# Raw words of w_out and of the last network loaded from POOL's queue, with earlier scalings and reads of h

## The chip, the cores and the metric

The kernel runs on one core of a Trainium2 chip. The metric is device time in microseconds. The core's engines each work through their own list of instructions in order: PE multiplies, DVE, ACT and POOL work element by element, SP does nothing but issue DMAs here. In the profile "SPq" is SP's queue and PEld the loading of weights into PE.

## What is computed

The reference, cut to what matters:

```python
# q, k, v: (4, 8, 576, 64), f: (4, 8, 576); all matrices of weights are float64
cum = cumsum(log(clip(f, 1e-4, 1)))
s = q @ k.T / 8 + cum[i] - cum[j]            # causal, -1e9 above the diagonal
p = exp(s - max(s)); p = p / (sum(p) + 1e-9)
x = (p @ v)                                  # as 2304 tokens x 512
h = x @ w_in                                 # 512 -> 2048
z = mish(h) @ w_out                          # 2048 -> 512
out = max(z @ w1, z @ w2, z @ w3) @ w_out2   # 512 -> 768 -> 512
```

## The kernel before

**Arithmetic.** Matmuls run in a reduced format, so each operand is split into a high and a low part and mm3 makes three products of them (lines 177 to 179: L177 is high by high, and so on for all matmuls of the networks). The weights lie in DRAM as float64. load_f32 brings their raw words (tile wr, or wr1 for the last network) by SP's queue (L150), and five DVE steps (L155 to L166) make float32 of them (tile wt; for w_in ACT does the first step). Then a split writes high and low part: for w_in on ACT and POOL, for all others on POOL alone (L138 the high, L142 the low). This whole is called a conversion below: 16 for w_in, 16 for w_out, 24 for w1 to w3, 6 for the last w_out. For w_in and w_out the raw words have two buffers, for the last network one.

**Attention.** Sixteen pairs of heads are worked through, each in three parts that overlap with the neighbours'. load() reads k, q, v and the decay rows (tile cb) and lets POOL mask cb (L285, L293). prep() splits and transposes q and k (tr). scores() multiplies them (sc), finds the row minima on DVE (mn), takes the exponential on ACT (L398), adds up and inverts the row sums on DVE (rr, L402, L403), and scales P on POOL (L405). av() transposes P (pp, L424), splits it (TA, TB) and multiplies by v (av); the result xt goes to DRAM (x_d, L462). A pair is done in two halves, g = 0 and g = 1.

**First network.** x_d is read in nine blocks of 256 tokens, split on POOL (xh, xl), and multiplied by w_in in 72 "h steps" of 24 matmuls; as many of them as are ready run between the parts of attention. ACT or DVE copies the result out of PSUM (he, L527 or L525), SP stores it (h_d, L529). In the "y phase" load_g reads h back (g, L610), applies Mish on ACT (L611) and splits it (gh on ACT, gl on DVE); 80 "y steps" of 12 matmuls by w_out add up y, which is copied to ze and stored as z_d. Two reads of h are asked for ahead of the step that uses them.

**Last network.** z_d is read (yr), split (yh, yl), and multiplied by w1, w2, w3 (tile wm; product g); the maximum goes to mx, is split (hh, hl) and multiplied by wo2 into o, copied to oe and stored.

**Order.** The order of the code is only a start: a scheduler that simulates the program arranges each engine's list. Work in a high_priority block is taken earlier, by the block's number; AHEAD is 3000. w_in is converted by a generator that the loop over attention calls (two conversions for each of the calls 7 to 14), those of w_out by the loop of the remaining h steps, and those of the last network by every second y step.

Of the kernel before, what the change touches and what calls it, by code (L numbers as in the profile page):

```python
# [32 lines left out]
BLK = 256  # L33
# [34 lines left out]
def tile_decay_attention__mish_ff__max3_ff(  # L68
# [38 lines left out]
    make_identity(nc, ident)  # L107
    identr = const.tile([128, 128], F32R, name="identr")
    nc.vector.tensor_copy(identr, ident)
# [33 lines left out]

    def load_f32(pool, srcs, bufs=None, abs_eng="dve", raw="wr"):

        m, n = len(srcs), srcs[0].shape[1]
        t = pool.tile([128, m, n], F32, name="wt", tag="wt", bufs=bufs)
        r = pool.tile([128, m, n, 2], I32, name=raw, tag=raw, bufs=bufs if raw == "wr" else 1)
        for i, src in enumerate(srcs):
            nc.sync.dma_start(r[:, i].rearrange("p n w -> p (n w)"), src.bitcast(I32))  # L150
        lo, hi, ti = r[:, :, :, 0], r[:, :, :, 1], t.bitcast(I32)
        if abs_eng == "act":
            nc.scalar.activation(t, hi.bitcast(F32), AF.Abs)
        else:
# [114 lines left out]
    def load(b, hp):  # L269
# [23 lines left out]
        nc.gpsimd.tensor_tensor(out=c4[:, 512:S], in0=c4[:, 512:S], in1=mask4, op=ALU.add)  # L293
# [16 lines left out]
    def prep(J):  # L310
# [35 lines left out]
        split_raw(J["vs"], raw[2], "act")  # L346
        J.update(q=(qh, ql), q4=last, k=kk)
# [13 lines left out]
    def scores(J, g):  # L361
# [11 lines left out]
        made = []  # L373
        for ci, (h, qt) in enumerate(tiles):
# [12 lines left out]
            for pi, (c0, w) in enumerate([(0, wd)] if qt < 4 else [(0, 288), (288, 288)]):  # L387
# [6 lines left out]
                    scale=-scale, scalar=(3e38 if pi == 0 else mn[:, ci:ci + 1]),  # L394
                    op0=ALU.add, op1=ALU.min, accum_out=mn[:, ci + pi:ci + pi + 1],
                )
            cl = ci + (qt == 4)
            nc.scalar.activation(  # L398
                Pt, Pt, AF.Exp, scale=-1.0, bias=mn[:, cl:cl + 1], accum_out=sm[:, ci:ci + 1],
            )  # L400
# [94 lines left out]
    def h_steps():  # L495
# [9 lines left out]
        for n, (i, fp) in enumerate(order):  # L505
# [48 lines left out]
    at.close()  # L554

# [51 lines left out]
    def load_g(ib, fp, a):  # L607
        n = blocks1[ib][1]
        g = gp_.tile([128, n], F32, name="g", tag="g")
        nc.sync.dma_start(g, h_d[ib][fp][:, a, :])  # L610
        nc.scalar.activation(g, g, AF.Mish)  # L611
        gh = gp_.tile([128, n], F32R, name="gh", tag="gh")
        gl = gp_.tile([128, n], F32R, name="gl", tag="gl")
        split(gh, gl, g, "act", "dve")
        return gh, gl

    wgen3 = load_w2()
    todo = [(ib, fp, a) for ib in range(len(blocks1)) for fp in range(NFP) for a in range(2)]
    ahead = [load_g(*todo[0]), load_g(*todo[1])]
    for step, (ib, fp, a) in enumerate(todo):  # L620
# [6 lines left out]
        final = fp == NFP - 1 and a == 1
        for j in range(KD):
            js = slice(j * 128, (j + 1) * 128)
            mm3(y[j], (wo[fp][:, 0, a, js], wo[fp][:, 1, a, js]), g, fp == 0 and a == 0, final)  # L630
# [94 lines left out]
```

## Time and profile before

| | us |
|---|---|
| median of 3 runs | 1039.22 (1038.8 to 1040.48) |
| the profiled execution | 1036.78 |
| its span | 1034.9 |
| time around the span | 1.9 |
| mean granted clock of PE | 0.962 |

The span is what the profiler sees from the first to the last instruction; the time is the whole execution. A busy PE needn't be PE at its peak: where the clock is lower, the same matmuls take longer. The stretches that the text uses are: 0 to 140 (attention's first pairs, nearly no h steps), 140 to 430.4 (attention with h steps between), to 520 (the last h steps beside the conversions of w_out), to 730 (the y phase, beside the conversions of the last network), and to the end (the last network).

### The profile page before, as it was taken

How to read it: one execution, taken by the hardware profiler on the slowest of the kernel's cores; microseconds unless marked ns; L12 is line 12 of the kernel's file. 1: busy time of each engine (PE TensorE's matmuls, PEld its weight loads, DVE VectorE, ACT ScalarE, POOL GpSimd, SP SyncE). 2: the span in 40 equal slices, each digit the busy share in tenths (PEclk: the TensorE clock that was granted, in tenths of full speed). 3: DMA queues.
4: the chain of work that ended last, by engine and by line, in shares of the span. 5: the costliest groups of instructions: out<-in, count | busy, mean ns of one | idle time of the engine just before them, and what ended most of it. 6: DMA issues, size and time to landing. Idle time of an engine off the chain costs nothing.

```text
span 1034.9 us, 15873 instructions
## 1 busy us (share of the span) xinstructions
PE 957.5 (93%) x5756; PEld 844.8 (82%) x5756; DVE 509.5 (49%) x1103; ACT 425.6 (41%) x936; POOL 379.9 (37%) x437
## 2 busy tenths in 40 slices
PE   4777789989998999899699989998999999999998
PEld 4655679989997999799688768778988888888886
DVE  4798885554555555599855776652211111111110
ACT  5777666565656566441133444434211211211111
POOL 6676784445445542365432423320111001011010
PEclk8888889999998999999899999998999999999999
DMA  6644544345344431485545555643300100200101
GB/s 158 175 145 143 174 155 129 120 131 150 119 129 120 139 107 63 146 285 168 175 141 195 180 185 163 203 134 102 103 21 1 61 21 1 82 1 1 41 0 41
DMA packets 106445, 119.15 MB, mean 115 GB/s; under 512 B 33984, under 2 KB 79552, under 8 KB 106368
## 3 DMA queue, kind: packets, MB, share of 16 engines
q1 hardware_dynamic: 106368, 118.15, 37.0%
q8 instruction: 45, 0.74, 0.3%
q14 instruction: 32, 0.26, 0.1%
HBM read 85.01 MB, written 33.10 MB: 114 GB/s over the span
## 4 chain that ended last, share of the span: by engine, by line
PE 54%; DMA 18%; DVE 17%; issue 4%; ACT 3%; POOL 3%; SPq 2%; DVEq 0%; POOLq 0%; ACTq 0%
PE g L179 7%; PE g L178 7%; PE g L177 7%; DMA wr<-in_moe_w_dram 5%; PE h L177 4%; PE h L178 4%; PE h L179 4%; DMA wr<-in_moe_w_out_dram 4%; DVE wt L162 3%; PE av L437 3%; PE pp L424 3%; PE sc L357 3%; DMA cb<-cum_d 3%; PE o L177 2%; PE o L179 2%
## 5 line engine op out<-in xcount | busy, mean ns | idle before, releaser
L177 PE MATMUL h<-xh,wi 128*128 128x256 f32 x576 | 168.5, 294 | 13.0 <-ACT he L527 7.9
L178 PE MATMUL h<-xl,wi 128*128 128x256 f32 x576 | 167.4, 291 | 1.9 <-POOL xl L142 1.9
L179 PE MATMUL h<-xh,wi 128*128 128x256 f32 x576 | 166.9, 290 | 0.0
L142 POOL TENSOR_TENSOR hl<-mx,hh 128x512 fp32r<-128x512 f32 x27 | 36.5, 1352 | 279.1 <-ACT hh L136 279.1
L177 PE MATMUL g<-yh,wm 128*128 128x512 f32 (+1 forms) x360 | 134.3, 373 | 0.0
L179 PE MATMUL g<-yh,wm 128*128 128x512 f32 (+1 forms) x360 | 134.3, 373 | 0.0
L178 PE MATMUL g<-yl,wm 128*128 128x512 f32 (+1 forms) x360 | 134.3, 373 | 0.0
L177 PE MATMUL y<-gh,wo 128*128 128x512 f32 (+1 forms) x320 | 118.6, 375 | 6.9 <-ACT gh L136 5.0
L177 PEld LDWEIGHTS h<-xh,wi 128*128 128x128 f32 x576 | 112.1, 195 | 15.2 <-ACT he L527 8.8
L178 PE MATMUL y<-gl,wo 128*128 128x512 f32 (+1 forms) x320 | 119.0, 373 | 2.9 <-DVE gl L142 2.8
L179 PE MATMUL y<-gh,wo 128*128 128x512 f32 (+1 forms) x320 | 118.2, 371 | 0.0
L178 PEld LDWEIGHTS h<-xl,wi 128*128 128x128 f32 x576 | 112.5, 195 | 3.2 <-POOL xl L142 2.1
L179 PEld LDWEIGHTS h<-xh,wi 128*128 128x128 f32 x576 | 112.2, 195 | 0.4
L611 ACT ACTIVATE g<-g 128x512 f32<-128x512 f32 (+1 forms) x80 | 46.8, 588 | 123.9 <-DMA g<-h_d 117.4
L681 DVE TENSOR_TENSOR mx<-g,mx 128x512 f32<-128x512 f32 x27 | 18.7, 692 | 156.3 <-PE g L179 156.3
L424 PE MATMUL pp<-ident,P 128*128 128x128 f32 x320 | 69.9, 314 | 21.9 <-POOL P L405 19.8
L398 ACT ACTIVATE P<-P,mn 128x128 f32<-128x128 f32 (+3 forms) x128 | 71.2, 557 | 39.2 <-DVE mn L392 38.5
L178 PEld LDWEIGHTS g<-yl,wm 128*128 128x128 f32 x360 | 67.9, 189 | 13.3
L179 PEld LDWEIGHTS g<-yh,wm 128*128 128x128 f32 x360 | 67.9, 189 | 13.2
L177 PEld LDWEIGHTS g<-yh,wm 128*128 128x128 f32 x360 | 67.9, 189 | 13.1
L405 POOL TENSOR_SCALAR P<-P,rr 128x128 f32<-128x128 f32 (+3 forms) x128 | 68.0, 550 | 25.7 <-DVE rr L403 12.5
L177 PEld LDWEIGHTS y<-gh,wo 128*128 128x128 f32 x320 | 61.3, 192 | 18.4 <-ACT gh L136 6.4
(101 smaller groups left out, 1982.9 us busy)
## 6 DMA issues: line engine op xcount, KB each, us to landing
h_d<-he SPq DMA_DIRECT2D x72, 256.0 KB, 3.5
g<-h_d SPq DMA_DIRECT2D x64, 256.0 KB, 3.2
wr<-in_moe_w_out_dram SPq DMA_DIRECT2D x22, 512.0 KB, 4.0
wr<-in_moe_w_dram SPq DMA_DIRECT2D x24, 384.0 KB, 3.2
cb<-cum_d SPq DMA_DIRECT2D x64, 128.0 KB, 3.2
wr<-in_moe_w_in_dram SPq DMA_DIRECT2D x32, 256.0 KB, 3.5
cb<-cum_d SPq DMA_DIRECT2D x32, 144.0 KB, 3.6
xr<-x_d SPq DMA_DIRECT2D x9, 512.0 KB, 4.0
```

The source lines that it names most:

```text
L142: eng.tensor_tensor(out=dst_lo, in0=src, in1=dst_hi, op=ALU.subtract)
L162: nc.vector.scalar_tensor_tensor(out=ti, in0=hi, scalar=-0x40000000, in1=ti, op0=ALU.bitwise_and, op1=ALU.bitwise_or,)
L177: nc.tensor.matmul(ps, wh, xh, start=start, stop=False, skip_group_check=True)
L178: nc.tensor.matmul(ps, wh, xl, start=False, stop=False, skip_group_check=True)
L179: nc.tensor.matmul(ps, wl, xh, start=False, stop=stop, skip_group_check=True)
L357: nc.tensor.matmul(o, lhs, rhs, start=n == 0, stop=n == len(mms) - 1, skip_group_check=True)
L398: nc.scalar.activation(Pt, Pt, AF.Exp, scale=-1.0, bias=mn[:, cl:cl + 1], accum_out=sm[:, ci:ci + 1],)
L405: nc.gpsimd.tensor_scalar(Pt, Pt, rr[:, ci:ci + 1], 1.0, op0=ALU.mult, op1=ALU.mult)
L424: nc.tensor.transpose(pp[:, n * 128:n * 128 + 128], Pt[:, k0:k0 + 128], ident)
L437: nc.tensor.matmul(avp[h][:, off:off + w], vl, T[:, i, c:c + w], start=kt == 0 and i == 0 and not (g == 0 and h == 1), stop=last and i == ...
L611: nc.scalar.activation(g, g, AF.Mish)
L681: nc.vector.tensor_tensor(out=mx, in0=g[1], in1=mx, op=ALU.max)
```

## The change

- The identity for PE's transposes (ident, identr) is built at a priority of 3 × AHEAD.
- load_f32 takes SP's queue only for w_in (pool wst), and POOL's for all other weights. The loads of w_in are issued after the newest store of x_d (a list of one, pace, which is emptied when attention ends).
- The masks on cb move from load() to the end of prep().
- In scores(), in the second half, the tile of the last 64 rows of both heads (None, 4) comes first and not last. rr and the scaling of P are done in two parts, each at a priority of 400, so that there are 64 small DVE instructions more.
- he that ACT copied is stored from ACT's queue, he that DVE copied from SP's; likewise ze.
- Reads of h run three ahead, at the priority AHEAD. The last block of 256 tokens is read two tiles in one, so there are 72 reads and not 80, and their tiles are always 512 wide.

Line numbers shift by up to 25: L150 is L156, L166 is L172, L138 and L142 are L139 and L143, L285 is L349, L405 is L389, L610 is L632 (L634 for the last block).

```diff
--- before.py
+++ after.py
@@ -104,9 +104,10 @@
-    make_identity(nc, ident)
-    identr = const.tile([128, 128], F32R, name="identr")
-    nc.vector.tensor_copy(identr, ident)
+    with tc.high_priority(3 * AHEAD):
+        make_identity(nc, ident)
+        identr = const.tile([128, 128], F32R, name="identr")
+        nc.vector.tensor_copy(identr, ident)
@@ -141,13 +142,18 @@ load_f32
-        for i, src in enumerate(srcs):
-            nc.sync.dma_start(r[:, i].rearrange("p n w -> p (n w)"), src.bitcast(I32))
+        queue = nc.sync if pool is wst else nc.gpsimd
+
+        with tc.issue_after(pace[-1].ins) if pace else ExitStack():
+            for i, src in enumerate(srcs):
+                queue.dma_start(r[:, i].rearrange("p n w -> p (n w)"), src.bitcast(I32))
@@ -281,16 +287,10 @@ load
-        for n, src, dst in ((2, 0, 5), (1, 3, 2), (1, 4, 4)):
-            nc.gpsimd.affine_select(
...
-        nc.gpsimd.tensor_tensor(out=c4[:, 512:S], in0=c4[:, 512:S], in1=mask4, op=ALU.add)
@@ -344,6 +344,13 @@ prep
         split_raw(J["vs"], raw[2], "act")
+        c2, c4 = J["cb"]
+        for n, src, dst in ((2, 0, 5), (1, 3, 2), (1, 4, 4)):
+            nc.gpsimd.affine_select(
...
+        nc.gpsimd.tensor_tensor(out=c4[:, 512:S], in0=c4[:, 512:S], in1=mask4, op=ALU.add)
@@ -367,10 +374,20 @@ scores
-        tiles = [(h, qt) for h in range(2) for qt in ((0, 1) if g == 0 else (2, 3))]
-        if g == 1:
-            tiles.append((None, 4))
+        tiles = [(None, 4)] if g == 1 else []
+        tiles += [(h, qt) for h in range(2) for qt in ((0, 1) if g == 0 else (2, 3))]
...
+        def scale_rows(part):
+
+            cs = slice(part[0], part[-1] + 1)
+            with tc.high_priority(400):
+                nc.vector.tensor_scalar(rr[:, cs], sm[:, cs], 1e-9, None, op0=ALU.add)
+                nc.vector.reciprocal(rr[:, cs], rr[:, cs])
+                for ci in part:
+                    nc.gpsimd.tensor_scalar(made[ci], made[ci], rr[:, ci:ci + 1], 1.0, op0=ALU.mult, op1=ALU.mult)
...
-        nt = len(tiles)
-        nc.vector.tensor_scalar(rr[:, :nt], sm[:, :nt], 1e-9, None, op0=ALU.add)
-        nc.vector.reciprocal(rr[:, :nt], rr[:, :nt])
-        for ci, Pt in enumerate(made):
-            nc.gpsimd.tensor_scalar(Pt, Pt, rr[:, ci:ci + 1], 1.0, op0=ALU.mult, op1=ALU.mult)
+            if ci == 2 - (g == 0):
+                scale_rows(list(range(ci + 1)))
+        scale_rows(list(range(3 - (g == 0), len(tiles))))
@@ -459,7 +474,7 @@ av
-            nc.sync.dma_start(x_d[blk][:, J["hp"], off:off + n], xt[:, done:done + n])
+            pace[:] = [nc.sync.dma_start(x_d[blk][:, J["hp"], off:off + n], xt[:, done:done + n])]
@@ -523,10 +538,12 @@ h_steps
                 nc.vector.tensor_copy(he, h)
+                queue = nc.sync
             else:
                 nc.scalar.activation(he, h, AF.Copy)
+                queue = nc.scalar
             ib, off = divmod(i * BLK, BLK2)
-            nc.sync.dma_start(h_d[ib][fp][:, :, off:off + BLK], he)
+            queue.dma_start(h_d[ib][fp][:, :, off:off + BLK], he)
@@ -605,29 +623,36 @@ load_g
+        g = gp_.tile([128, BLK2], F32, name="g")
...
+        if n == BLK2:
+            nc.sync.dma_start(g, h_d[ib][fp][:, a, :])
+        else:
+            nc.sync.dma_start(g.rearrange("p (a n) -> p a n", a=2), h_d[ib][fp][:])
...
-    ahead = [load_g(*todo[0]), load_g(*todo[1])]
+    with tc.high_priority(AHEAD):
+        ahead = [load_g(*t) for t in todo[:3]]
...
-        if step + 2 < len(todo):
-            ahead.append(load_g(*todo[step + 2]))
...
+        if step + 3 < len(todo):
+            with tc.high_priority(AHEAD):
+                ahead.append(load_g(*todo[step + 3]))
@@ -635,9 +660,10 @@
                 if j % 2:
                     nc.vector.tensor_copy(ze, y[j])
+                    nc.sync.dma_start(z_d[ib][:, j, :], ze)
                 else:
                     nc.scalar.activation(ze, y[j], AF.Copy)
-                nc.sync.dma_start(z_d[ib][:, j, :], ze)
+                    nc.scalar.dma_start(z_d[ib][:, j, :], ze)
```

Where instructions stand now. First, POOL and the conversions in the y phase (wm is a weight of the last network, wt its float32, wr its raw words). POOL's list before:

```order
L138 TENSOR_SCALAR wm_6704<-wt 128x384
L142 TENSOR_TENSOR wm_6704<-wt,wm_6704 128x384
L138 TENSOR_SCALAR wm_6704<-wt 128x384
L142 TENSOR_TENSOR wm_6704<-wt,wm_6704 128x384
L138 TENSOR_SCALAR wm_6705<-wt 128x384
L142 TENSOR_TENSOR wm_6705<-wt,wm_6705 128x384
```

POOL's list after:

```order
L139 TENSOR_SCALAR wm_6767<-wt 128x384
L156 DMA wr_6937<-in_moe_w_dram 128x768
L143 TENSOR_TENSOR wm_6767<-wt,wm_6767 128x384
L139 TENSOR_SCALAR wm_6768<-wt 128x384
L156 DMA wr_6985<-in_moe_w_dram 128x768
L143 TENSOR_TENSOR wm_6768<-wt,wm_6768 128x384
```

The next load of raw words now stands between a conversion's high and low split; before, it was on SP, between reads of h.

Second, SP's queue in attention, at the first loads of w_in. Before, six of them stand behind the store of the first pair's x_d (rawk, rawq, rawv and cb are the loads of the next pairs):

```order
L462 DMA x_d_60<-xt_441 128x256
L292 DMA cb_491<-cum_d 64x576 x2
L150 DMA wr<-in_moe_w_in_dram 128x512 x6
L248 DMA rawk<-in_k_dram 128x2x256
L253 DMA rawk<-in_k_dram 64x64 x2
```

After, the first four stand behind a store of the third pair:

```order
L254 DMA rawq<-in_q_dram 128x2x256
L259 DMA rawq<-in_q_dram 64x64 x2
L477 DMA x_d_60<-xt_959 128x256
L156 DMA wr<-in_moe_w_in_dram 128x512 x4
L254 DMA rawk<-in_k_dram 128x2x256
```

Of the 16 conversions of w_in 1, 5, 8, 11, 14 and 16 stood ahead of the ends of pairs one to six on DVE; now 0, 0, 0, 4, 9 and 13 do, and 16 by the seventh.

Third, DVE's list at the end of the y phase. Before, the last conversion of all is over while gl of the last block are still to come:

```order
L162 SCALAR_TENSOR_TENSOR wt<-wr_8213,wt 128x512
L142 TENSOR_TENSOR gl<-g,gh 128x256
L166 SCALAR_TENSOR_TENSOR wt<-wr_8213,wt 128x512
L142 TENSOR_TENSOR gl<-g,gh 128x256 x2
L637 COPY ze<-y_7931 128x512
L637 COPY ze<-y_7933 128x512
L142 TENSOR_TENSOR gl<-g,gh 128x256 x13
```

After, three conversions are left when y is copied out; the first of them is here:

```order
L662 COPY ze<-y_8382 128x256
L662 COPY ze<-y_8384 128x256
L707 TENSOR_TENSOR mx<-g_8647,mx 128x512
L161 TENSOR_SCALAR wt<-wr_8188 128x512
L162 TENSOR_SCALAR wt<-wt 128x512
L165 TENSOR_SCALAR wt<-wt 128x512
L168 SCALAR_TENSOR_TENSOR wt<-wr_8188,wt 128x512
L708 TENSOR_TENSOR mx<-g_8648,mx 128x512
L172 SCALAR_TENSOR_TENSOR wt<-wr_8188,wt 128x512
```

In the y phase itself both lists have about one conversion for two gl; the last three conversions moved behind y, among the maxima of the last network's first block.

## Rows read from the trace of the kernel before

**Rows 1.** The page: span, busy time of each engine, chain that ended last

```profile
span 1034.9 us, 15873 instructions
...
PE 957.5 (93%) x5756; PEld 844.8 (82%) x5756; DVE 509.5 (49%) x1103; ACT 425.6 (41%) x936; POOL 379.9 (37%) x437
...
PE 54%; DMA 18%; DVE 17%; issue 4%; ACT 3%; POOL 3%; SPq 2%; DVEq 0%; POOLq 0%; ACTq 0%
```

**Rows 2.** Windows: stretch, length, busy us (instructions) by engine, clock, DMA share, GB/s

```profile
0.00:140.00 140.00, 97.92 (x559) 81.10 (x560) 106.17 (x266) 95.16 (x234) 100.20 (x130) 0.84 0.56 163
140.00:430.40 290.40, 278.95 (x2259) 272.61 (x2257) 164.50 (x458) 174.63 (x432) 137.17 (x183) 0.98 0.39 118
430.40:520.00 89.60, 79.24 (x592) 76.97 (x593) 73.75 (x98) 22.52 (x38) 44.31 (x39) 0.92 0.67 211
520.00:730.00 210.00, 200.23 (x967) 167.84 (x966) 118.55 (x225) 82.73 (x156) 61.77 (x60) 0.98 0.50 159
730.00:753.50 23.50, 23.50 (x198) 23.50 (x197) 6.04 (x7) 6.44 (x7) 4.18 (x2) 1.00 0.36 113
753.50:1034.90 281.40, 277.63 (x1190) 222.79 (x1188) 40.49 (x52) 44.19 (x69) 32.32 (x25) 1.00 0.07 25
```

**Rows 3.** Timeline of DVE: start, us, engine, line, tile; attention's last xt

```profile
429.26 1.11 DVE L454 TENSOR_TENSOR xt<-av,vlo 64x320 f32<-64x320 f32 x4 [1.57 <-ACT vlo L445]
```

**Rows 4.** What PE waited for, 0 to 140: us in total, times, longest

```profile
PE pp L424 <- POOL P L405: 14.5, 14, 3.4
PE tr L319 <- DVE identr L109: 7.6, 1, 7.6
PE tr L319 <- POOL qk L142: 5.3, 3, 3.1
PE sc L357 <- ACT qh L334: 5.0, 3, 2.3
```

**Rows 5.** Timeline of SP's queue, 130 to 152

```profile
135.83 13.26 SPq L150 DMA_DIRECT2D wr<-in_moe_w_in_dram  x6
149.18 0.39 SPq L248 DMA_DIRECT2D rawk<-in_k_dram  x1
```

**Rows 6.** Timeline of POOL, 316 to 334; in brackets the idle before, and its releaser

```profile
325.10 1.51 POOL L285 TENSOR_SCALAR_AFFINE_SELECT cb<-cb 128x512 f32<-128x512 f32 x3 [7.36 <-DMA cb<-cum_d]
326.60 2.49 POOL L405 TENSOR_SCALAR P<-P,rr 128x384 f32<-128x384 f32 x4
```

**Rows 7.** Timeline of PE, 326 to 332

```profile
327.25 0.47 PE L424 MATMUL pp<-ident,P 128*128 128x128 f32 x1 [3.64 <-POOL P L405]
```

**Rows 8.** Timeline of ACT, 500 to 513

```profile
508.70 0.63 ACT L611 ACTIVATE g<-g 128x512 f32<-128x512 f32 x1 [9.69 <-DMA g<-h_d]
```

**Rows 9.** Timeline of SP's queue, 590 to 603: loads of raw words

```profile
591.23 0.33 SPq L150 DMA_DIRECT2D wr<-in_moe_w_dram  x1
...
596.84 0.33 SPq L150 DMA_DIRECT2D wr<-in_moe_w_dram  x1
```

**Rows 10.** DMA issues: in and out, count, KB each, median us from issue to landing

```profile
wr<-in_moe_w_dram SPq DMA_DIRECT2D x24, 384.0 KB, 3.2
```

**Rows 11.** Timeline of DVE, 590 to 603

```profile
591.12 1.59 DVE L142 TENSOR_TENSOR gl<-g,gh 128x512 fp32r<-128x512 f32 x2
594.47 0.36 DVE L155 TENSOR_SCALAR wt<-wr 128x384 int32<-128x384 int32 x1 [1.76 <-DMA wr<-in_moe_w_dram]
```

**Rows 12.** Line L142: count, min/median/max ns, first and last start us

```profile
L142 POOL TENSOR_TENSOR wm<-wt,wm x24: 1007/1018/1538, 520.6 to 656.4; 128x384 fp32r<-128x384 f32 x24
```

**Rows 13.** Timeline of POOL, 652 to 682: the 27th conversion's high split

```profile
677.22 0.99 POOL L138 TENSOR_SCALAR wo<-wt 128x512 fp32r<-128x512 f32 x1 [4.91 <-DVE wt L166]
```

**Rows 14.** Timeline of POOL, 590 to 603

```profile
596.90 0.89 POOL L138 TENSOR_SCALAR wm<-wt 128x384 fp32r<-128x384 f32 x1 [3.31 <-DVE wt L166]
...
602.51 0.51 POOL L138 TENSOR_SCALAR wm<-wt 128x384 fp32r<-128x384 f32 x1 [3.32 <-DVE wt L166]
```

**Rows 15.** Timeline of SP's queue, 129: the longest issue of one transfer there

```profile
129.09 0.63 SPq L260 DMA_DIRECT2D rawv<-in_v_dram  x1
```

More of the change, by code (lines that the diff above doesn't have):

```diff
@@ L142, in split @@
         eng.tensor_tensor(out=dst_lo, in0=src, in1=dst_hi, op=ALU.subtract)
+    pace = []
     def load_f32(pool, srcs, bufs=None, abs_eng="dve", raw="wr"):
@@ L283, in load @@
             nc.sync.dma_start(c2[:, h, 3:5, :], src[:, 2:4])
-        for n, src, dst in ((2, 0, 5), (1, 3, 2), (1, 4, 4)):
-            nc.gpsimd.affine_select(
-                out=c2[:, :, dst:dst + n, :], in_=c2[:, :, src:src + n, :], pattern=[[0, 2], [0, n], [-1, 128]],
-                compare_op=ALU.is_ge, fill=-1e30, base=0, channel_multiplier=1,
-            )
         ld(rv, v, b, hp, False)
@@ L346, in prep @@
         split_raw(J["vs"], raw[2], "act")
+        c2, c4 = J["cb"]
+        for n, src, dst in ((2, 0, 5), (1, 3, 2), (1, 4, 4)):
+            nc.gpsimd.affine_select(
+                out=c2[:, :, dst:dst + n, :], in_=c2[:, :, src:src + n, :], pattern=[[0, 2], [0, n], [-1, 128]],
+                compare_op=ALU.is_ge, fill=-1e30, base=0, channel_multiplier=1,
+            )
+        nc.gpsimd.tensor_tensor(out=c4[:, 512:S], in0=c4[:, 512:S], in1=mask4, op=ALU.add)
         J.update(q=(qh, ql), q4=last, k=kk)
@@ L369, in scores @@
         rr = aw.tile([128, 5], F32, name="rr", bufs=4)
-        tiles = [(h, qt) for h in range(2) for qt in ((0, 1) if g == 0 else (2, 3))]
-        if g == 1:
-            tiles.append((None, 4))
+        tiles = [(None, 4)] if g == 1 else []
+        tiles += [(h, qt) for h in range(2) for qt in ((0, 1) if g == 0 else (2, 3))]
         made = []
+        col = 0
+        def scale_rows(part):
[5 more added lines that the diff above has]
+                    nc.gpsimd.tensor_scalar(made[ci], made[ci], rr[:, ci:ci + 1], 1.0, op0=ALU.mult, op1=ALU.mult)
         for ci, (h, qt) in enumerate(tiles):
@@ L393, in scores @@
                     out=like(Pt[:, c0:c0 + w]), in0=like(sc[:, :w]), in1=cb[pi],
-                    scale=-scale, scalar=(3e38 if pi == 0 else mn[:, ci:ci + 1]),
-                    op0=ALU.add, op1=ALU.min, accum_out=mn[:, ci + pi:ci + pi + 1],
+                    scale=-scale, scalar=(3e38 if pi == 0 else mn[:, col - 1:col]),
+                    op0=ALU.add, op1=ALU.min, accum_out=mn[:, col:col + 1],
                 )
-            cl = ci + (qt == 4)
+                col += 1
             nc.scalar.activation(
-                Pt, Pt, AF.Exp, scale=-1.0, bias=mn[:, cl:cl + 1], accum_out=sm[:, ci:ci + 1],
+                Pt, Pt, AF.Exp, scale=-1.0, bias=mn[:, col - 1:col], accum_out=sm[:, ci:ci + 1],
             )
-        nt = len(tiles)
-        nc.vector.tensor_scalar(rr[:, :nt], sm[:, :nt], 1e-9, None, op0=ALU.add)
-        nc.vector.reciprocal(rr[:, :nt], rr[:, :nt])
-        for ci, Pt in enumerate(made):
-            nc.gpsimd.tensor_scalar(Pt, Pt, rr[:, ci:ci + 1], 1.0, op0=ALU.mult, op1=ALU.mult)
+            if ci == 2 - (g == 0):
+                scale_rows(list(range(ci + 1)))
+        scale_rows(list(range(3 - (g == 0), len(tiles))))
         return P
@@ L554, in tile_decay_attention__mish_ff__max3_ff @@
     at.close()
+    pace.clear()
     sb = ExitStack()
@@ L607, in load_g @@
     def load_g(ib, fp, a):
+        g = gp_.tile([128, BLK2], F32, name="g")
+        gh = gp_.tile([128, BLK2], F32R, name="gh")
+        gl = gp_.tile([128, BLK2], F32R, name="gl")
         n = blocks1[ib][1]
-        g = gp_.tile([128, n], F32, name="g", tag="g")
-        nc.sync.dma_start(g, h_d[ib][fp][:, a, :])
+        if n == BLK2:
+            nc.sync.dma_start(g, h_d[ib][fp][:, a, :])
+        else:
+            nc.sync.dma_start(g.rearrange("p (a n) -> p a n", a=2), h_d[ib][fp][:])
         nc.scalar.activation(g, g, AF.Mish)
-        gh = gp_.tile([128, n], F32R, name="gh", tag="gh")
-        gl = gp_.tile([128, n], F32R, name="gl", tag="gl")
         split(gh, gl, g, "act", "dve")
-        return gh, gl
+        return [(t, (gh[:, i * n:(i + 1) * n], gl[:, i * n:(i + 1) * n])) for i, t in enumerate([a] if n == BLK2 else [0, 1])]
     wgen3 = load_w2()
-    todo = [(ib, fp, a) for ib in range(len(blocks1)) for fp in range(NFP) for a in range(2)]
-    ahead = [load_g(*todo[0]), load_g(*todo[1])]
+    todo = [(ib, fp, a) for ib, (_, n) in enumerate(blocks1) for fp in range(NFP) for a in range(n // BLK)]
+    with tc.high_priority(AHEAD):
+        ahead = [load_g(*t) for t in todo[:3]]
     for step, (ib, fp, a) in enumerate(todo):
@@ L623, in tile_decay_attention__mish_ff__max3_ff @@
             y = [yps.tile([128, n], F32, name=f"y{j}", tag="y") for j in range(KD)]
-        g = ahead.pop(0)
-        if step + 2 < len(todo):
-            ahead.append(load_g(*todo[step + 2]))
[L627 to L630, printed above, removed]
+        parts = ahead.pop(0)
+        if step + 3 < len(todo):
+            with tc.high_priority(AHEAD):
+                ahead.append(load_g(*todo[step + 3]))
+        for t, g in parts:
+            final = fp == NFP - 1 and t == 1
+            for j in range(KD):
+                js = slice(j * 128, (j + 1) * 128)
+                mm3(y[j], (wo[fp][:, 0, t, js], wo[fp][:, 1, t, js]), g, fp == 0 and t == 0, final)
         if step % 2:
```

## The prediction

> **What bounds the kernel now.** Read the page's first lines first: PE is busy 957.5 of 1034.9 us, so the kernel can shorten only where PE waits or where its clock is low [rows 1]. The chain that ended last is PE for 54%, but DMA for 18% and DVE for 17%: something else leads in some stretches [rows 1]. The busy times by stage say where [rows 2]. In the first 140 us PE idles 140 − 97.9 = 42.1 us at clock 0.84. In the rest of attention it idles 290.4 − 279.0 = 11.5. From attention's end (430.4, the last xt [rows 3]) to 520 it idles 10.4, from 520 to 730 9.8. From 730 on, where the last network runs, it idles 3.8 in 304.9. So there are 74 us to be had before 730, and hardly any after.
>
> Then the waits. Early, PE waits most for POOL's scaling of P (14.5 us), for identr (7.6), for the splits of q and k (5.3 and 5.0) [rows 4]. SP has the cause of some of it: six raw loads of w_in hold its queue for 13.26 us, and the next rawk goes out only at 149.18 [rows 5]. Later in attention the masks do it: at 325.10 POOL waits 7.36 us for cb, masks it, and only at 326.60 scales P, for which PE has stood 3.64 us [rows 6, 7]. After attention one knot stands out: at 508.70 ACT has waited 9.69 us for a read of h [rows 8]; behind that Mish, on the same engine, stands the copy of h out of PSUM without which PE can't begin the next h step.
>
> In the y phase (520 to 730) a second chain runs beside PE, and it matters for this change. There is one buffer for the raw words of the last network. SP issues a load at 591.23 and the next at 596.84: 5.61 us [rows 9], which is the load (3.2, [rows 10]) and the five conversion steps on DVE. DVE fills part of the flight with two gl (1.59 us), then stands 1.76 us for the words [rows 11]. PE's two y steps, fed by those two gl, are about as long, so chain and PE run level. Over the phase the chain goes at (656.4 − 520.6)/23 = 5.90 us [rows 12], and its 27th conversion ends at 677.2 [rows 13], that is 246.8 after attention's end.
>
> **The change, part by part.**
>
> *Attention.* Building identr first takes some of the 7.6 us away: I take 1.5, since PE's first matmul needs the split of k as well, which is loaded first. Scaling in two parts and masks moved behind the next pair's splits: half of the 14.5, so 7. Loads of w_in held back until the third pair's x_d is stored, so that rawk, rawq and cb are not queued behind them: half of the 10.3 of the q and k waits, so 5. Gain 13.5. Against it, the 16 conversions of w_in now lie in pairs four to seven (4, 9, 13 and 16 of them done at those ends in the order; 11, 14, 16 and 16 before); DVE is 57% busy after 140 [rows 2], so most fits, and I give back 3.5: 10 net. After 140 the masks and scalings take some 4.5 of the 11.5 idle. Attention then ends at 430.4 − 14.5 = 416. Both ends: nothing (430) and, if three quarters of the 53.6 us idle go less the give-back, some 36 (394); I keep 405 to 428, as an early stall that goes leaves another behind it. The 64 added DVE instructions on rr (two small ones more per half pair) and the added POOL starts lie in this same idle time.
>
> *Reads of h, three ahead and put forward; stores of h and z from ACT's queue.* They act on the knot [rows 8]. If all idle after attention went (10.4 + 9.8 = 20.2), y would end at 416 + 299.6 − 20.2 = 416 + 279.4. An issue takes 0.33 to 0.63 us on SP [rows 9, 15], and ACT makes 56 now; it is busy 22.5 of 90 and 83 of 210 there [rows 2], so that is hidden. What is late next is the conversion chain.
>
> *Raw loads from POOL's queue.* Removed from SP: the issue itself and the queueing behind reads of h that wait for gl; the chain's 5.90 against 5.61 is that, about 0.3 us each, 7 in 23. Added: in the order POOL does the high split of conversion k, then issues load k+1, then the low split. SP issued as the last conversion step ended (596.84, the same moment at which POOL's high split starts, 596.90 [rows 9, 14]); POOL can issue only after that split, 0.89 us beside gl, 0.51 without [rows 14]. To this comes what POOL needs for an issue, which no row shows, since SP issues everything. Its bounds: 0 (as quick as SP) and 2.3 (the load takes as long again as 3.2, less 0.89). I take 0.6, the longest issue of one transfer without a wait that SP shows (0.63, [rows 15]), so 1.5 us per load in all; range 0.5 to 3.2. The low split now stands behind the issue, and its reader, PE, comes far later.
>
> The w_out loads have two buffers, so a later landing is half hidden: 16 × 0.25 = 4 us. Then the 27th conversion ends at 416 + 246.8 + 4 − 7 + 27 × 1.5 = 416 + 284. DVE works in order and does one conversion for every two gl, to the end of y in the new order too; so y ends one step behind, at 416 + 288, not at the 279 that PE alone would allow. The last three conversions stand among the maxima of the first block of the last network (23.5 us, [rows 2]), and the last one's splits end some 2.5 us behind it. So o begins at 416 + 288 + 26 = 730 (753.5 before), and the rest is 281.4, unchanged [rows 2]: span 1011.4. The profiled run was 1036.8 for a span of 1034.9; plus 1.9 this gives 1013, to be set against 1036.8, and, as the median of the runs is 2.4 above the profiled one, 1013 to 1016 as a median. I forecast 1014.
>
> The Trainium skill (DMA: Bandwidth & Descriptors, Anatomy of one DMA) gives 2.0 us + bytes/436e3 for a load from GpSimd's queue, an estimate of 2.9 us for 384 KB, less than the 3.2 that the row has for SP's; by it the split alone would remain, and the sum would be the cheap case's 1005, below. No row here shows such a load.
>
> **Rivals.**
>
> *The loads cost nothing.* At 1.15 us per load or less PE sets the end of y: 416 + 279.4 + 26 + 281.4 + 1.9 = 1005. For it: the split alone is 0.5 to 0.9. Against: the issue must then cost under 0.3.
>
> *The issue waits for DVE.* Behind each conversion DVE runs two gl of 1.59 us together [rows 11], and POOL slows beside them (0.89 against 0.51, [rows 14]). If the issue gets through only when they are done, a load comes 1.6 + 0.6 = 2.2 later: y ends at 416 + 307, time 1032. The Trainium skill has this as a rule (SBUF — State Buffer, the box on DVE blocking DMA): GpSimd can't write descriptors while DVE holds the port that they share, and such loads belong on ACT's or SP's queue. Whether gl is such an operation no row tells; the slower split beside it agrees.
>
> *Slower: the chain throttles y.* With 3.2 us more per load the period is 9.1 us, gl comes at that pace, and PE stands 3 us in every two y steps: 416 + 333 + 26 + 281.4 + 1.9 = 1059. It loses from 2.35 us per load on, as 27 × 0.85 = 23 is what the rest gives. For it: only that a single buffer leaves no cover, 1.76 us idle on DVE being all the slack.
>
> *The early gain isn't there* (w_in comes too late, h steps starve, or the masks are merely late elsewhere): attention ends at 430, time 1028.
>
> **How the numbers follow.** Forecast 0.45 (1000 to 1025), cheap loads 0.2, issue behind DVE 0.12, early gain gone 0.08, slower 0.15. Two tenths left out at the ends: 996 (cheap, attention at 407) to 1045 (part of the slow case). A measurement tells 0.2% (2 us). Faster 0.78: the first, second and fourth case whole and some half of the third; slower 0.17; same 0.05.
>
> **What would show it.** Right: first PE matmul by 6.2; SP's six-load row gone; attention over by 405 to 428; no 9.69 us wait of ACT at Mish; raw loads 6.8 to 7.4 us apart in the y phase, DVE's wait for words 3 us instead of 1.76, with PE idle 1 to 1.5 us in two y steps; o first at 718 to 742. Wrong: periods above 8 us (slow), or below 6.2 (cheap), or attention at 430. The size rests on one price that no row has, POOL's issue; 0.5 us there moves the end by 13.5 us.

## The result

The changed kernel takes 1025.45 us (median of 4 runs, 1024.19 to 1027.7) against 1039.01 of the kernel before (median of 4): a ratio of 0.9873 (0.9853 to 0.9893), 13.6 us faster. The forecast was 1014, faster, with a range from 996 to 1045. Direction and range held; the gain is about half of the 25 us forecast. The two halves of the sum missed in opposite directions, attention by 7 us to the good and the y phase by 24 to the bad, so that the time lies in the range is partly luck.

The page after (its first two lines, the queue that is new, and the chain that ended last; compare [rows 1]):

```profile
span 1025.9 us, 15858 instructions
...
PE 953.6 (93%) x5756; PEld 836.3 (82%) x5756; DVE 521.1 (51%) x1159; ACT 420.8 (41%) x920; POOL 398.8 (39%) x483
...
q0 software_dynamic: 5088, 20.97, 6.5%
...
PE 56%; DMA 17%; DVE 15%; issue 4%; POOL 3%; ACT 3%; SPq 2%; DVEq 0%; ACTq 0%; POOLq 0%
```

The windows by stage (columns as in [rows 2]; here attention ends at 408.6, y at 720.3, and o begins at 744.6):

```profile
0.00:140.00 140.00, 105.78 (x664) 88.75 (x664) 109.19 (x284) 96.78 (x240) 100.03 (x130) 0.87 0.53 152
140.00:408.60 268.60, 260.92 (x2157) 256.00 (x2157) 173.01 (x504) 170.64 (x426) 139.47 (x185) 1.00 0.45 133
408.60:490.00 81.40, 77.46 (x606) 75.91 (x605) 58.89 (x76) 21.74 (x36) 41.06 (x45) 0.98 0.65 213
490.00:720.30 230.30, 207.59 (x944) 168.52 (x943) 122.31 (x218) 81.00 (x142) 72.71 (x88) 0.96 0.46 148
720.30:744.60 24.30, 24.30 (x205) 24.30 (x204) 14.25 (x23) 6.62 (x8) 10.82 (x11) 1.00 0.48 152
744.60:1025.90 281.30, 277.58 (x1190) 222.79 (x1188) 43.48 (x58) 44.07 (x69) 34.71 (x28) 1.00 0.07 25
```

| | before | after | difference |
|---|---|---|---|
| attention ends | 430.4 | 408.6 | −21.8 |
| from there to the end of y | 299.4 | 311.7 | +12.3 |
| from there to the first o | 23.7 | 24.3 | +0.6 |
| from there to the end | 281.4 | 281.3 | −0.1 |
| span | 1034.9 | 1025.9 | −9.0 |

Attention gained more than forecast, and the y phase, which was to gain 11 us, lost 12. There PE idles 230.3 − 207.6 = 22.7 us, where before it idled 9.8 from 520 on.

### The profile page after: what moved, and what is told of

It is laid out like the page before. It is cut to its first block, busy times and chain, and to the rows that moved or that the text cites. A ratio compares the mean times of both kernels' runs of the same rounds, so it can differ in the third digit from the quotient of the medians.

```text
span 1025.9 us, 15858 instructions
## 1 busy us (share of the span) xinstructions
PE 953.6 (93%) x5756; PEld 836.3 (82%) x5756; DVE 521.1 (51%) x1159; ACT 420.8 (41%) x920; POOL 398.8 (39%) x483
## 3 DMA queue, kind: packets, MB, share of 16 engines
q0 software_dynamic: 5088, 20.97, 6.5%
## 4 chain that ended last, share of the span: by engine, by line
PE 56%; DMA 17%; DVE 15%; issue 4%; POOL 3%; ACT 3%; SPq 2%; DVEq 0%; ACTq 0%; POOLq 0%
DMA wr<-in_moe_w_dram 8%; PE g L185 7%; PE g L184 7%; PE g L183 7%; PE h L184 4%; PE h L185 4%; PE h L183 4%; PE av L452 4%; PE sc L364 4%; PE o L183 2%; DVE wt L168 2%; PE o L185 2%; PE o L184 2%; PE pp L439 2%; DVE wt L172 2%
## 5 line engine op out<-in xcount | busy, mean ns | idle before, releaser
L183 PE MATMUL h<-xh,wi 128*128 128x256 f32 x576 | 166.0, 289 | 5.3 <-ACT he L543 3.9
L185 PE MATMUL h<-xh,wi 128*128 128x256 f32 x576 | 165.1, 287 | 0.0
L184 PE MATMUL y<-gl,wo 128*128 128x512 f32 (+1 forms) x320 | 122.9, 384 | 17.6 <-DVE gl L143 17.6
L183 PE MATMUL y<-gh,wo 128*128 128x512 f32 (+1 forms) x320 | 122.4, 383 | 5.1 <-DVE ze L662 3.2
L143 POOL TENSOR_TENSOR hl<-mx,hh 128x512 fp32r<-128x512 f32 x27 | 34.8, 1290 | 225.9 <-ACT hh L137 225.9
L185 PE MATMUL y<-gh,wo 128*128 128x512 f32 (+1 forms) x320 | 120.1, 377 | 0.0
L183 PEld LDWEIGHTS h<-xh,wi 128*128 128x128 f32 x576 | 110.6, 193 | 6.8 <-ACT he L543 4.1
L185 PEld LDWEIGHTS h<-xh,wi 128*128 128x128 f32 x576 | 110.6, 192 | 0.3
L635 ACT ACTIVATE g<-g 128x512 f32<-128x512 f32 x72 | 45.3, 631 | 141.7 <-DMA g<-h_d 130.8
L184 PEld LDWEIGHTS y<-gl,wo 128*128 128x128 f32 x320 | 62.8, 196 | 33.7 <-DVE gl L143 24.1
L143 DVE TENSOR_TENSOR gl<-g,gh 128x512 fp32r<-128x512 f32 x72 | 59.8, 832 | 39.4 <-ACT gh L137 39.3
```

The costliest lines, as they stand in the source:

```text
L143: eng.tensor_tensor(out=dst_lo, in0=src, in1=dst_hi, op=ALU.subtract)
L183: nc.tensor.matmul(ps, wh, xh, start=start, stop=False, skip_group_check=True)
L184: nc.tensor.matmul(ps, wh, xl, start=False, stop=False, skip_group_check=True)
L185: nc.tensor.matmul(ps, wl, xh, start=False, stop=stop, skip_group_check=True)
```

## The experiments

All ratios are against the kernel before, run beside each; it took 1036.7 to 1039.0 us there, so ratios compare better than times. "y lasts" counts from attention's end, the last h steps included. "Pace" is the number of matmuls that PE did in 160 us of the y phase, the count behind PE's busy time in one window (520 to 680 in kernels whose attention ends before 420, 540 to 700 in the others). "gl behind gh" is the mean time in us from the end of gh on ACT to the start, on DVE, of the gl that is made of it, over the gl of 512 columns that start at least 80 us after attention's end (58 to 67 in each trace):

| kernel | time, us | ratio (95%) | attention ends | y lasts from there | pace | gl behind gh |
|---|---|---|---|---|---|---|
| before | 1039.0 | | 430.4 | 299 | 674 | 0.54 |
| after | 1025.5 | 0.9873 (0.9853 to 0.9893) | 408.6 | 312 | 611 | 1.55 |
| e_attn | 1027.9 | 0.9900 (0.9870 to 0.9930) | 416.7 | 305 | 643 | 0.83 |
| e_nopace | 1038.3 | 1.0004 (0.9984 to 1.0023) | 424.5 | 305 | 616 | 1.59 |
| e_reads | 1039.0 | 1.0022 (1.0005 to 1.0040) | 430.2 | 300 | 647 | 0.74 |
| e_oldread | 1027.1 | 0.9907 (0.9887 to 0.9927) | 411.2 | 308 | 630 | 1.29 |
| e_bpool | 1044.2 | 1.0074 (1.0048 to 1.0099) | 429.3 | 307 | 631 | 1.31 |
| e_sp | 1024.5 | 0.9875 (0.9858 to 0.9893) | 412.2 | 308 | 621 | 0.99 |
| e_first | 1033.7 | 0.9974 (0.9954 to 0.9995) | 411.5 | 315 | 609 | 1.48 |
| e_two | 1033.7 | 0.9958 (0.9944 to 0.9972) | 411.1 | 316 | 556 | 1.73 |
| e_share_ord | 1017.9 | 0.9831 (0.9780 to 0.9883) | 411.0 | 299 | 646 | 0.80 |
| e_share_ord_g6 | 1014.0 | 0.9778 (0.9729 to 0.9827) | 411.4 | 294 | 654 | 0.90 |
| e_share_spord | 1002.0 | 0.9662 (0.9614 to 0.9710) | 410.1 | 287 | 697 | 0.24 |
| e_share_spord_g6 | 1003.1 | 0.9666 (0.9641 to 0.9690) | 415.2 | 281 | 726 | 0.30 |

The windows behind the paces of before, after, e_two, e_share_ord and e_share_spord, in this order:

```profile
540.00:700.00 160.00, 153.80 (x674) 124.94 (x673) 101.44 (x187) 63.49 (x113) 54.29 (x52) 1.00 0.54 174
```
```profile
520.00:680.00 160.00, 146.55 (x611) 115.77 (x610) 80.91 (x154) 60.23 (x105) 46.87 (x58) 0.97 0.47 152
```
```profile
520.00:680.00 160.00, 136.74 (x556) 103.42 (x555) 128.91 (x187) 58.38 (x102) 66.14 (x81) 0.98 0.53 169
```
```profile
520.00:680.00 160.00, 151.48 (x646) 120.11 (x645) 112.45 (x188) 62.90 (x110) 61.87 (x78) 0.99 0.53 174
```
```profile
520.00:680.00 160.00, 156.11 (x697) 127.36 (x696) 109.60 (x188) 68.00 (x119) 45.91 (x51) 0.99 0.56 182
```

Busy times mislead here: from before to after PE's falls by 5% and its matmuls by 9%. The granted clock was lower in that window (0.97 and not 1.00): PE ran three stretches of 3.4 us at 1.2 and not 2.4 GHz, each begun within 2 us of a wait for gl of 1.5 to 2.0 us, and a y matmul starts 0.43 us after the one before it there and 0.23 elsewhere (windows as above; the clock is the third number from the end):

```profile
540.60:544.00 3.40, 3.40 (x9) 2.48 (x9) 2.43 (x5) 1.83 (x4) 0.22 (x1) 0.50 0.71 239
557.60:561.00 3.40, 3.40 (x9) 2.66 (x8) 1.89 (x4) 0.73 (x2) 1.95 (x3) 0.50 0.53 186
591.80:595.20 3.40, 3.40 (x11) 3.01 (x12) 1.69 (x2) 2.41 (x5) 1.86 (x3) 0.50 0.55 187
```

Across all 14 kernels the pace goes with the last column: where gl comes late behind gh, PE does less.

**The parts alone.** First, attention's part only (identity, held-back loads of w_in, masks, scalings), the rest as before:

```diff
-        queue = nc.sync if pool is wst else nc.gpsimd
+        queue = nc.sync
...
-                queue = nc.scalar
+                queue = nc.sync
...
-        if step + 3 < len(todo):
-            with tc.high_priority(AHEAD):
-                ahead.append(load_g(*todo[step + 3]))
+        if step + 2 < len(todo):
+            ahead.append(load_g(*todo[step + 2]))
```

> The attention part of the change alone (identity first, loads of w_in held back, masks behind the splits, scaling in two parts); queues, reads of h and stores as before. Theory (the whole gain is attention's, and reads put forward and POOL's queue only cost): attention ends at 408 to 412, y some 299 us later as before, time 1014 to 1020, faster than the whole change. Rival (the early end is lost again in the knot behind attention, which only the reads undo): 1025 to 1035.

Measured 1027.9, ratio 0.9900: attention alone gives some 10 of the 13.6 us. By its number the rival held, but not by its reason: the early end (416.7, a little later than expected) was partly lost behind attention, where y took 305 us instead of 299, and the loss isn't in the knot. The last h matmul comes 87 us after attention's end and not 91; behind it the pace is lower, 643, with PE waiting 6.9 us for gl and not 2.8. The order of DVE's list differs from that of before there too.

The holding back, undone alone:

```diff
-        with tc.issue_after(pace[-1].ins) if pace else ExitStack():
+        with ExitStack():
```

> The changed kernel with the loads of w_in not held back. Theory (holding them back is what frees the first pairs, 16.6 us for the second pair in place of 24.4): attention ends some 10 us later, time 1033 to 1038. Rival (masks, scalings and identity do it): 1023 to 1028.

Measured 1038.3, as slow as before: without it the whole gain is gone. Attention ends at 424.5, so holding the loads back is worth 16 of its 22 us in these two profiles, the other parts of attention 6; against the other kernels with the changed kernel's order in attention, which end it at 410 to 415, it is 9 to 14. The last start of an xt instruction (line L469; count, min/median/max, first and last start), after and then this kernel:

```profile
L469 DVE TENSOR_TENSOR xt<-av,vlo x96: 217/336/484, 33.6 to 408.3; 64x256 f32<-64x256 f32 x32, 64x128 f32<-64x128 f32 x32, 64x320 f32<-64x320 f32 x16, 64x64 f32<-64x64 f32 x16
```
```profile
L469 DVE TENSOR_TENSOR xt<-av,vlo x96: 217/340/485, 33.4 to 424.2; 64x256 f32<-64x256 f32 x32, 64x128 f32<-64x128 f32 x32, 64x320 f32<-64x320 f32 x16, 64x64 f32<-64x64 f32 x16
```

The new reads of h, put into the kernel before (load_g and its loop as after, nothing else):

> The kernel before with the new reads of h alone (three ahead, put forward, last block read in pairs). Theory: the y phase gets slower, 3.2 us a step for 2.8, the knot behind attention goes: y ends some 305 us after attention, time 1040 to 1047. Rival (reads are a gain, as the knot and the waits for gh go): 1020 to 1034.

Measured 1039.0, ratio 1.0022. Neither: the pace falls (674 to 647), and what the knot behind attention gives back (the last h matmul comes 85 us after attention and not 91) nearly pays for it; 0.22% is 2 us. The reverse, the changed kernel with the old reads:

> The changed kernel with the reads of h as before (two ahead, not put forward). Theory (the reads put forward cost some 8 us in the y phase, since DVE's order then puts fewer gl behind each conversion's end): 1014 to 1020. Rival (reads cost nothing, POOL's loads alone set the pace): 1024 to 1030.

Measured 1027.1, ratio 0.9907 against 0.9873 with intervals that overlap: no difference that can be told. The pace rises from 611 to 630; the time doesn't follow. Either way the reads are worth no more than a few us.

POOL's queue, put into the kernel before:

```diff
-            nc.sync.dma_start(r[:, i].rearrange("p n w -> p (n w)"), src.bitcast(I32))
+            (nc.sync if pool is wst else nc.gpsimd).dma_start(r[:, i].rearrange("p n w -> p (n w)"), src.bitcast(I32))
```

> The kernel before with only the queue of w_out and of the last network's raw loads changed to POOL's. Theory: the period is that of the changed kernel, 8.2 us, y ends some 311 us after attention, which ends at 430 as before: about 1049 (1042 to 1056), slower. Rival (the queue change is itself a gain, since SP is free for reads of h): 1025 to 1036.

Measured 1044.2, 0.74% slower: the direction of the theory, three quarters of its 10 us. This is the sum of a gain and a loss. Up to the last h matmul PE idles 2.3 us behind attention where it idled 10.4, and that matmul comes 79 us after attention and not 91; from there to the end of y PE idles 20.3 us where it idled 9.8, and the pace falls by 43 of 674 matmuls. With only the queue edited, gl comes 1.31 us behind gh and not 0.54.

**Undoing the queue in the changed kernel.** The theory at this point was the prediction's: the chain of load and conversion sets the pace, and POOL's queue lengthens it.

```diff
-        queue = nc.sync if pool is wst else nc.gpsimd
+        queue = nc.sync
```

> The changed kernel with all raw loads on SP's queue again. Theory (in the y phase the time is set by the chain of raw load and conversion, and POOL's queue lengthens a load): the period of the conversions falls from 8.3 to about 6.1 us, y ends some 285 us after attention and not 312, time about 1000 (995 to 1008). Rival (SP's queue, full of reads of h, would hold the loads up as much, so POOL's queue costs nothing net): 1020 to 1030.

Measured 1024.5: no change. The conversions did come faster, every 6.5 us on average and not every 8.3, but the pace hardly did (621 for 611), and y took 308 us for 312 where 285 was expected. DVE's wait for the words of w1 to w3 fell little (515 to 720, after and then this kernel):

```profile
DVE wt L161 <- DMA wr<-in_moe_w_dram: 61.4, 21, 5.6
```
```profile
DVE wt L161 <- DMA wr<-in_moe_w_dram: 52.2, 20, 4.5
```

So the chain's length alone doesn't set the y phase, and the theory in this form fell. What does, a stretch of this kernel shows; ACT, DVE and PE (start, duration, engine, line, tile; in brackets the idle before and its releaser):

```profile
535.38 0.62 ACT L137 ACTIVATE gh<-g 128x512 fp32r<-128x512 f32 x1
```
```profile
536.86 0.36 DVE L161 TENSOR_SCALAR wt<-wr 128x384 int32<-128x384 int32 x1 [3.06 <-DMA wr<-in_moe_w_dram]
537.25 0.36 DVE L162 TENSOR_SCALAR wt<-wt 128x384 f32<-128x384 f32 x1
537.65 0.36 DVE L165 TENSOR_SCALAR wt<-wt 128x384 int32<-128x384 int32 x1
537.93 0.68 DVE L143 TENSOR_TENSOR gl<-g,gh 128x512 fp32r<-128x512 f32 x1
```
```profile
538.66 0.50 PE L184 MATMUL y<-gl,wo 128*128 128x512 f32 x1 [0.75 <-DVE gl L143]
```

gh is there at 536.0, and DVE is free. But the gl made of it stands fourth in DVE's list, behind the first three steps of a conversion, and the first of these waits until 536.86 for its raw words. So gl ends at 538.61 and not at 536.7, and PE, which came to that step at 537.5, waits 0.75 us. The conversion takes the gl hostage, so to say. Of the 66 gl of the last column 17 stood ready in this way for over 0.5 us while DVE idled, in this kernel as in the changed one. That is the smaller part of it: of the 66 us by which these gl start behind their gh here DVE idles 26 and spends 38 on steps of conversions that its list has ahead of them; in the changed kernel it is 31 and 60 of 102. How many gl stand beside a conversion, and where, is the scheduler's choice, and it changes with the queue: between the first and the last low split of w1 to w3 the changed kernel has 59 gl to 23 periods, about five to two, and this one 47, about four to two. So a shorter period came with fewer gl in it, and the time for one gl is 3.2 us in both.

The place of the load on POOL, tested by putting it ahead of the high split:

```diff
-            for i, src in enumerate(srcs):
+            with ExitStack() if pool is wst else tc.high_priority(AHEAD):
...
```

> The changed kernel with the loads still on POOL's queue, but each put ahead of the high split of the conversion that frees its buffer. Theory: the place behind the split costs 0.5 to 0.9 us of each load's 2.1, so the period falls to about 7.5 and the time to 1004 (998 to 1012). Rival (the whole price is POOL's slower issue and landing, the place is free): 1020 to 1028.

Measured 1033.7, slower than both theories said. The load goes out 0.36 us sooner behind the last conversion step (0.49 for 0.85 on average), but its words land only 0.25 sooner (4.8 us for 5.0), so this says little about the chain's length. The conversions come at 7.7 us for 8.3 because there are more of them to a gl in the new order; the pace is 609. What makes it slower lies ahead of the y phase, at 497 (what PE waited for, 412 to 760; it waited 3.9 us for he in the changed kernel):

```profile
PE h L184 <- ACT he L544: 12.1, 3, 10.0
```

Two buffers for the last network's raw words (with two for ze, for room):

```diff
-        r = pool.tile([128, m, n, 2], I32, name=raw, tag=raw, bufs=bufs if raw == "wr" else 1)
+        r = pool.tile([128, m, n, 2], I32, name=raw, tag=raw, bufs=bufs if raw == "wr" else 2)
...
-    zst = sb.enter_context(tc.tile_pool(name="zst", bufs=4, side="right", reuse_waits="tile"))
+    zst = sb.enter_context(tc.tile_pool(name="zst", bufs=2, side="right", reuse_waits="tile"))
```

> The changed kernel with two buffers for the last network's raw words (and two for ze instead of four, for room). Theory: a late landing is hidden, the chain no longer sets the y phase, PE does: y ends some 280 us after attention, time 993 to 1003. Rival (DVE's order, one conversion for two gl and gl waiting for ACT's gh, throttles y by itself): above 1015.

Measured 1033.7, as the rival said. DVE hardly waits for words any more, it is full (108.5 of 120 us from 520 to 640), because the conversions, ready sooner, are placed ahead of gl: 96 of the 116 us by which gl starts behind gh go to their steps. PE waits for gl longer than in any other kernel (what DVE waited for, 515 to 720, and what PE waited for, 412 to 760: total, times, longest):

```profile
DVE wt L161 <- DMA wr<-in_moe_w_dram: 4.3, 4, 2.7
```
```profile
PE y L184 <- DVE gl L143: 26.4, 25, 6.1
```

**Order and buffers together.** If conversions ahead of a ready gl are the cause, two buffers and an order that puts each conversion behind the newest gl must free PE. The raw words of the last network share w_out's two buffers, which are idle by then, so that nothing else shrinks:

```diff
-        r = pool.tile([128, m, n, 2], I32, name=raw, tag=raw, bufs=bufs if raw == "wr" else 1)
+        r = pool.tile([128, m, n if m > 1 else 512, 2], I32, name="wr", tag="wr", bufs=bufs)[:, :, 0:n]
...
-        split(gh, gl, g, "act", "dve")
+        last_gl[:] = [split(gh, gl, g, "act", "dve")]
...
         if step % 2:
-            next(wgen3, None)
+            with tc.issue_after(last_gl[-1].ins):
+                next(wgen3, None)
```

(split returns its second instruction for this.)

> The changed kernel with two buffers for the last network's raw words (it shares the two of w_out) and with each conversion queued on DVE behind the newest gl. Theory one (a conversion's first step waits for its raw words ahead of a gl that is ready, and DVE works in order): y steps of 2.8 us in place of 3.3, y ends some 285 us after attention, time 1000 to 1008. Theory two (the ring read, Mish, gh, gl, next read over few buffers sets the pace): steps stay at 3.05 or more, time 1015 to 1028.

> As the first of these, with the raw loads on SP's queue. With two buffers the load's length is hidden, so by theory one the queue makes no difference: 1000 to 1008. If SP's loads, queued among reads of h, hold the reads up: 5 us or more above the first.

> The same with six buffers instead of four for what is read of h, so that a read waits for an older gl. Theory one: no further gain, 1000 to 1008 as the kernel beside it. Theory two: this and not the other brings the step to 2.8 us, 1000 to 1010, 10 us or more under the kernel beside it.

Measured 1017.9 on POOL's queue, 1002.0 on SP's, 1014.0 on POOL's with six buffers for g. By its number theory two has the first, theory one the second, neither the third. Against e_two, order (and the full number of ze buffers) is worth some 13 us by the ratios. The queue is worth another 16, which neither theory said: with two buffers the landing is hidden, and yet POOL's loads cost. What PE waited for from 408 to 720, on SP's queue:

```profile
PE h L183 <- ACT he L543: 7.1, 1, 7.1
PE y L183 <- ACT ze L667: 1.8, 2, 1.3
PE y L184 <- DVE gl L143: 1.5, 4, 0.7
```

The wait for gl is 1.5 us. It was this before (430 to 730), in the changed kernel (490 to 745) and in e_share_ord (408 to 720):

```profile
PE y L178 <- DVE gl L142: 2.8, 4, 1.2
```
```profile
PE y L184 <- DVE gl L143: 17.6, 15, 4.6
```
```profile
PE y L184 <- DVE gl L143: 10.4, 8, 4.7
```

No run has the order with one buffer, or two buffers on SP's queue without the order, so what each is worth by itself isn't shown. The last run adds the six buffers to this kernel:

```diff
-        g = gp_.tile([128, BLK2], F32, name="g")
+        g = gp_.tile([128, BLK2], F32, name="g", bufs=6)
```

> The fastest so far (two raw buffers, conversions behind gl, raw loads on SP's queue) with six buffers for what is read of h. If the ring of reads still holds the y phase at 2.83 us a step, it falls to about 2.75, y ends 280 us after attention, time 994 to 999. If PE sets the pace already, no change: 1000 to 1004.

Measured 1003.1, no change in time, so 1002 to 1003 is what this line of work gives: 3.4% under the kernel before, some 22 us under the changed one. In its profile the pace did rise (726 for 697; about 15 of the 726 are due to the last block, whose matmuls are half as wide and begin at 670), but attention ended 5 us later in the same order. In the kernels with one and the same order in attention, the changed one among them, its end varies from 408.6 to 415.2, so differences of 5 us in a single profile say little.

## Why the prediction was right, and where it was not

*Attention: 14.5 us forecast, 21.8 measured (about 19 in the other kernels of that order).* Right in kind, and the weights were wrong. For the first 140 us the forecast gave identr 1.5, masks and scalings 7, the held-back loads 5. The holding back gave the most, 9 to 16 in all by e_nopace. What PE waited for, 0 to 140, after (compare [rows 4]):

```profile
PE tr L319 <- POOL qk L143: 13.9, 4, 7.5
PE pp L439 <- POOL P L389: 8.8, 9, 2.5
PE sc L364 <- DVE mn L409: 4.2, 5, 2.2
PE sc L364 <- ACT qh L334: 2.7, 3, 1.3
```

The wait for P fell by 5.7 us from 14.5 to 8.8 (a fall of 7 was forecast), that for qh from 5.0 to 2.7. The 7.6 us for identr are gone by name alone: PE's first matmul starts at 7.55 where it started at 7.63. The 1.5 that was taken became 0.08, since the split of k on POOL, named as next, ends then; the wait for such splits grew from 5.3 to 13.9, of which 7.5 are this one:

```profile
7.55 1.39 PE L319 MATMUL tr<-identr,qk 128*128 128x128 f32 x9 [7.55 <-POOL qk L143]
```

The second pair of heads now takes 16.6 us instead of 24.4, with no conversion of w_in beside it. The forecast put this down to SP's queue. In e_nopace, where loads and conversions are back, PE waits as long for the splits of q and k on POOL (13.8) but 9.5 us for DVE's minima (mn) where it waits 4.4 here, which points to DVE being free; queue and engines aren't separated by any run.

*Price of a load on POOL: 1.5 us forecast, 1.7 measured.* This was the term without a row, and it came out: from the end of a conversion's last step to the landing of the next words 4.9 us pass and not 3.2 (medians over w1 to w3). POOL's list, an issue behind the high split, and the loads' landing:

```profile
591.22 0.88 POOL L139 TENSOR_SCALAR wm<-wt 128x384 fp32r<-128x384 f32 x1 [6.29 <-DVE wt L172]
592.05 0.58 POOL L156 DMA_DIRECT2D wr<-in_moe_w_dram  x1
592.66 1.02 POOL L143 TENSOR_TENSOR wm<-wt,wm 128x384 fp32r<-128x384 f32 x1
```
```profile
wr<-in_moe_w_dram POOLq DMA_DIRECT2D x24, 384.0 KB, 4.0
```

The split takes 0.8 on average, and from issue to landing 4.0 pass instead of 3.2 [rows 10]. The issue itself is 0.58 (0.6 was taken from SP's longest). The Trainium skill's fit for such loads (DMA: Bandwidth & Descriptors, Anatomy of one DMA) gives an estimate of 2.9 us; the trace says 4.0, and it decides. The Trainium skill also has such loads wait for their descriptors while DVE runs an operation in a two-port mode (SBUF — State Buffer, the box on DVE blocking DMA). No run here settles whether that happens beside a gl: in the changed kernel the five issues beside one took 0.59 us and landed 4.5 us after their start on average, the 19 others 0.58 and 4.2; in e_oldread it is 4.5 (seven) and 3.8, in e_first 4.2 for twenty beside one, and single landings overlap.

*The step that failed: the period of the conversions, and that it sets the end of y.* The sum had 5.9 − 0.3 + 1.5 = 7.1 us a conversion. It came to (698.3 − 507.9)/23 = 8.28, 2.4 more than before [rows 12] and not 1.2 (line L143: count, min/median/max ns, first and last start):

```profile
L143 POOL TENSOR_TENSOR wm<-wt,wm x24: 1011/1025/1037, 507.9 to 698.3; 128x384 fp32r<-128x384 f32 x24
```

DVE's wait for words was as forecast, 61.4 us in 21 waits or 2.9 each, where 3 was expected. What was wrong is "one conversion for every two gl": the new order has 59 gl to 23 periods, the old one 45, so the period grew with the gl in it, and the time for one gl only from 3.0 to 3.2 us. The 27th conversion ends (starts its high split) 314.7 us after attention and not 284, and y ends with it, at 311.7 and not 288:

```profile
723.30 0.62 POOL L139 TENSOR_SCALAR wo<-wt 128x512 fp32r<-128x512 f32 x1 [4.77 <-DVE wt L172]
```

But y doesn't end there because the 27th conversion does. In e_sp, where y ends as late (719.9), the 27th is over 46 us before that:

```profile
673.68 1.00 POOL L139 TENSOR_SCALAR wo<-wt 128x512 fp32r<-128x512 f32 x1 [5.46 <-DVE wt L172]
```

So the sum took conversions and gl as one chain, in which less load is less time, and e_sp and e_two, with shorter periods, show that it isn't: PE is paced by gl, and gl by what stands ahead of it in DVE's list. The gain from the reads ahead, which together with this loss made the forecast of 288, didn't come either: e_reads and e_oldread show the new reads as neutral within a few us. The knot [rows 8] moved more than it went. ACT still waits 11.19 us for a read of h, at 506.83, but no h step stands behind it any more; PE waits there for gl (4.6 us, at 504.2) and not for he (7.7 before, at 509.9).

```profile
506.83 0.63 ACT L635 ACTIVATE g<-g 128x512 f32<-128x512 f32 x1 [11.19 <-DMA g<-h_d]
```

*Rivals.* "The issue waits for DVE" (1032) didn't happen in the form given: POOL issues 0.83 us after its split starts, and the words land 4.0 us later. By the prediction's own sign, a period above 8 us, it was the slow case that came, and part of its mechanism is right, PE paced by gl; its reason, the load's length, isn't, and its price of some 45 us was far too high. e_bpool measures the queue in the kernel before as +7.6 us of median. "The early gain isn't there" is refuted by attention's end at 408.6, and at 416.7 in e_attn.

*What stays open.* Why POOL's queue costs 16 us with two buffers. Both loads land in time there. POOL is busier by 16 us in the 160 of the window (61.9 against 45.9), nearly all of it the issues. A gl that overlaps POOL's low split takes up to 2.4 us for 0.69, here 1.46 in e_share_ord:

```profile
609.14 1.03 POOL L143 TENSOR_TENSOR wm<-wt,wm 128x384 fp32r<-128x384 f32 x1
```
```profile
609.27 1.46 DVE L143 TENSOR_TENSOR gl<-g,gh 128x512 fp32r<-128x512 f32 x1 [1.30 <-ACT gh L137]
```

That alone doesn't separate the queues: from 520 to 680 17 of 51 gl overlap the low split and nothing else of POOL's in e_share_ord and 18 of 54 in e_share_spord, and they take 1.4 and 1.3 us on average. But the next read of h waits for such a gl, and the round from gl through read, Mish and gh to the gl after the next is about as long as PE's two steps, 5.4 us (5.5 around the gl shown), so a small difference may tell. That six buffers for g give back 4 us agrees with it; the intervals overlap, and it isn't shown. Nor is it shown why the order in e_attn, with the queue and the reads of before, has gl later behind gh than before (0.83 and 0.54).

## What to carry to other kernels

Where an engine works through its list in order and serves two customers, look at what stands in the list ahead of the instruction that the critical engine waits for: a step that waits for a transfer, or work that nobody needs yet. Shortening the transfer gave nothing here while the order stayed bad (e_sp), and a second buffer alone made it worse (e_two); buffer, order and queue together gave some 22 us. Moving a load to another queue also changed the scheduler's order, so such a run tests two things at once. When an early stall is named after the last thing waited for, ask what ends next: here identr hid the split of k, which ended 0.08 us earlier.

## What the runs showed of the hardware

A load from POOL's queue takes POOL 0.58 us of its own time and lands 0.8 us later than one of the same size from SP's for 384 KB (4.0 against 3.2 us, medians from the start of the issue) and 0.3 later for 512 KB (4.3 against 4.0); SP's issue takes 0.33. Its packets are listed under a queue of their own kind (software_dynamic), 20.97 MB of them. A gl on DVE (two inputs) took up to 2.4 us beside POOL's low split (two inputs too), where it takes 0.69 alone; beside the high split (one input; 14 gl in the changed kernel from 520 to 680) or beside an issue alone (19 in e_first) it took 0.68 to 0.69.
